# The sign of a weight word from ScalarE instead of VectorE, for 20 of 32 pieces

## The chip, the cores and the metric

The kernel runs on one core of a Trainium2 chip. The metric is the device time of one execution in microseconds, the median of several. The engines are TensorE (PE, matrix products), VectorE (DVE), ScalarE (ACT), GpSimd (POOL) and SyncE (SP, which here issues DMAs).

## What is computed

The reference is attention with a local window and a few global keys, then a two-layer network with a gelu:

```python
batch, n_heads, seq, head_dim = (4, 8, 768, 64)
n_tokens, d_model, d_ff = (3072, 512, 2048)
...
scores = scale * q @ k.T + bias        # bias: minus slope times distance
scores = where(is_global | is_local, scores, -1e9)
a = softmax(scores)
x = (a @ v)  as (3072, 512)
h = x @ w_in                            # (3072, 2048)
g = 0.5 * h * (1.0 + erf(h / sqrt(2)))
return (g @ w_out).astype(float32)
```

The weights w_in and w_out are 64-bit floats. The chip has none, so each weight arrives as two 32-bit words and has to be decoded into a 32-bit float, and then into two 16-bit floats (a high and a low part) for TensorE.

## The kernel before

The tokens go in 12 chunks of 256 (`NCH`), the 2048 columns of the hidden layer in 8 slices of 256 (`NST`). A step is one chunk with one slice: products with w_in, gelu, products with w_out. The method `run` walks over the steps and emits for each the products of the next step, the gelu, the attention of later chunks and the loads. The first two chunks are interleaved slice by slice, and while they run the weights are decoded; from the third chunk on all weights lie decoded in SBUF. The table `DECODE` says at which step each piece is decoded. The attention of a chunk consists of scores (`scores_pair`, reduced on VectorE in line 511), exponentials (`exps`, line 545, ScalarE), the reciprocal and the normalising (`norm`, lines 554 to 563; VectorE for the first two chunks, POOL for later ones), transposes (`flip`, line 584, TensorE, copied by ScalarE in line 589) and the products with v (`av_pair`, line 658), of which ScalarE makes the high half of x and VectorE the low half (line 212). Counted products of zeros (`FILL`, `warm`) keep TensorE busy between the products of the first attention.

A piece of weights is 128 x 512 words of 64 bits; there are 4 in a slice and 32 in all. `load_words` fetches it by SP (line 223) into one of 4 buffers of the pool `ws` or 3 of the pool `stg`. `split_weights` decodes it: the low word is scaled to a small integer in place (line 250 on POOL for slices 0 and 1, `s < POOLED`; line 252 on ScalarE for slices 2 to 7); VectorE shifts the high word's lower bits up (line 258), puts its two top bits in front (line 261) and adds the low word (line 263). A step later `part_weights` lets ScalarE make the high 16-bit part (line 273) and VectorE the low one (line 213).

The order on each engine is not the order of the text: a planner simulates the engines as it goes and places every instruction by that. The method `after` ties an instruction behind another without a wait; `behind` ties a VectorE instruction behind the last reduction of earlier steps, and `last_table` ties a ScalarE instruction behind the last exponential or gelu of earlier steps, because ScalarE loads another table (1.28 us in the trace) at each change between these two. Between engines, a reader of a tile waits by a semaphore for its writer.

Of the kernel before, what the change touches and what calls it, by code (L numbers as in the profile page):

```python
# [10 lines left out]
F16 = mybir.dt.float16  # L11
I32 = mybir.dt.int32
U32 = mybir.dt.uint32
AF = mybir.ActivationFunctionType
ALU = mybir.AluOpType
# [42 lines left out]
POOLED = 2  # L58
# [60 lines left out]
class Fast:  # L119
# [115 lines left out]
    def split_weights(self, s, i):  # L235
        nc = self.nc
        if i == 0:
            if s == LATE:
                self.early.close()
                self.wts = self.ctx.enter_context(self.tc.tile_pool(name="wlate", bufs=1, side="right"))  # L240
            if s == NST - 1:
                self.words.close()
                self.wts = self.ctx.enter_context(self.tc.tile_pool(name="wlast", bufs=1))
            for nm, dst, shape in (("win", self.win, [P, 4, 256]), ("wout", self.wout, [P, 2, 512])):
                dst[s] = tuple(self.wts.tile(shape, F16, name=f"{nm}{k}{s}") for k in "hl")
            self.sw[s] = self.wts.tile([P, 2, 4, 256], F16, name=f"sw{s}")
        w = self.raw.pop((s, i, "w"))
        lw, hw = w[:, :, 0], w[:, :, 1]
        if s < POOLED:
            nc.gpsimd.tensor_scalar(out=lw, in0=lw.bitcast(U32), scalar1=2.0 ** -29, scalar2=None, op0=ALU.mult)  # L250
        else:
            ins = nc.scalar.activation(out=lw, in_=lw.bitcast(U32), func=AF.Copy, scale=2.0 ** -29).ins
            if len(self.his) > 1:
                self.after(ins, self.his[-2], "a piece begins when ScalarE is through with the last but one")
            if self.last_table is not None:
                self.after(ins, self.last_table, "a piece comes behind the exponentials of earlier steps")
        a = self.sm.tile([P, 512], I32, name=f"wb{s}_{i}", tag="o", bufs=3)
        ins = nc.vector.tensor_scalar(out=a, in0=hw, scalar1=0x07FFFFFF, scalar2=3,
                                      op0=ALU.bitwise_and, op1=ALU.logical_shift_left)
        self.behind(ins)  # L260
        nc.vector.scalar_tensor_tensor(out=a, in0=hw, scalar=-0x40000000, in1=a,
                                       op0=ALU.bitwise_and, op1=ALU.bitwise_or)
        nc.vector.tensor_tensor(out=a, in0=a, in1=lw, op=ALU.add)  # L263
        self.words_of[s, i] = a

# [977 lines left out]
```

## Time and profile before

| | us |
|---|---|
| median of 3 runs | 616.1 (615.17, 616.1, 620.82) |
| profiled execution | 614.87 |
| its span, first to last instruction | 613.1 |
| PE busy | 594.8 (97%) |
| DVE busy | 478.6 (78%) |
| ACT busy | 351.2 (57%) |
| POOL busy | 94.3 (15%) |

The busy time is the share of the span in which an engine worked. TensorE's products are pipelined and their ends are modelled, so its busy time is no measure of how well it is used, but its idle time and what ended it can be read. The weights are decoded between 12 and 125 us of the span.

### The profile page before, as it was taken

To read this page: it belongs to the slowest core of one execution; us is meant where nothing else is said; L and a number is where in the kernel's file an instruction comes from. 1 tells how busy PE (TensorE), PEld (TensorE's weight loads), DVE (VectorE), ACT (ScalarE), POOL (GpSimd) and SP (SyncE) were. 2 spreads that over 40 slices of the span, in tenths; PEclk is the share of its full clock that TensorE was granted. 3 is DMA by queue.
4 is the path that set the end of the run, shared out by engine and by line. 5 is a ranking of instruction groups with operands and counts; after the bars stand their busy time and mean duration, and the time that the engine had idled before them with its cause. 6 is when DMAs were issued, how large, how long until landed. Compare 5 with 4: busy or idle time off the path is not lost.

```text
span 613.1 us, 18033 instructions
## 1 busy us (share of the span) xinstructions
PE 594.8 (97%) x7320; PEld 451.6 (74%) x7320; DVE 478.6 (78%) x1490; ACT 351.2 (57%) x817; POOL 94.3 (15%) x196
## 2 busy tenths in 40 slices
PE   8988999999999999999999999999999999999995
PEld 5655544445666666888888888888888888888884
DVE  7999999977658865767966966976976976975885
ACT  3686577685636736547557556556566466463331
POOL 2240006311303111022022022022022022020000
PEclk9999999999999999999999999999999999999999
DMA  8969826443531364183184184194294194100001
GB/s 260 236 235 257 274 96 207 113 78 104 127 79 52 77 154 120 44 217 122 41 220 124 37 223 122 70 220 127 72 218 129 69 212 136 69 3 2 35 1 40
DMA packets 106618, 77.00 MB, mean 126 GB/s; under 512 B 54176, under 2 KB 94112, under 8 KB 106528
## 3 DMA queue, kind: packets, MB, share of 16 engines
q1 hardware_dynamic: 103952, 72.11, 42.4%
q10 hardware_dynamic: 2576, 3.67, 1.8%
q8 instruction: 59, 0.97, 0.7%
q14 instruction: 31, 0.25, 0.1%
HBM read 69.47 MB, written 6.29 MB: 124 GB/s over the span
## 4 chain that ended last, share of the span: by engine, by line
PE 60%; DVE 21%; ACT 10%; DMA 4%; issue 2%; SPq 1%; POOL 1%; ACTq 0%; DVEq 0%; POOLq 0%
PE h L717 23%; PE seven L793 16%; PE acc L883 7%; ACT n L545 4%; PE av L615 4%; DVE ss L757 3%; PE s L449 3%; PE h L711 3%; PE acc L868 2%; DMA w<-w 2%; DMA kr<-kT 2%; ACT L545 2%; DVE x L212 2%; DVE gl L213 2%; DVE wb L263 1%
## 5 line engine op out<-in xcount | busy, mean ns | idle before, releaser
L717 PE MATMUL h<-x,winh 128*128 128x256 f16 x1344 | 225.7, 273 | 1.7 <-DVE x L212 1.7
L717 PE MATMUL h<-x,winl 128*128 128x256 f16 x672 | 183.1, 273 | 0.0
L717 PEld LDWEIGHTS <-winh 128*128 128x128 f16 x1344 | 129.2, 98 | 24.2 <-issue 4.0
L563 POOL TENSOR_SCALAR n<-n,su 128x160 f32<-128x160 f32 (+1 forms) x160 | 77.4, 504 | 411.3 <-DVE su L557 270.0
L759 ACT ACTIVATE sh<-ss 128x512 f16<-128x512 f32 x64 | 40.3, 630 | 70.5 <-DVE ss L757 70.5
L752 ACT ACTIVATE gr<-h 128x512 f32<-128x512 f32 x64 | 38.2, 597 | 65.8 <-PE h L717 63.1
L717 PEld LDWEIGHTS <-winl 128*128 128x128 f16 x672 | 65.8, 98 | 8.9 <-issue 1.3
L213 DVE SCALAR_TENSOR_TENSOR gl<-gr,gh 128x384 f16<-128x384 f32 (+1 forms) x96 | 57.4, 598 | 12.4 <-ACT gh L854 12.0
L793 PE MATMUL seven<-sw,sh 128*128 128x256 f16 x384 | 66.9, 273 | 0.0
L545 ACT ACTIVATE n<-n,mn 128x160 f32<-128x160 f32 x144 | 59.6, 415 | 1.8 <-DVE mn L460 1.6
L757 DVE TENSOR_TENSOR ss<-gr 128x128 f32<-128x128 f32 x128 | 31.1, 284 | 32.3 <-ACT gr L752 32.3
L793 PEld LDWEIGHTS <-sh 128*128 128x128 f16 x512 | 50.1, 98 | 5.8
L793 PE MATMUL seven<-sw,sl 128*128 128x256 f16 x192 | 52.3, 273 | 0.1
L213 DVE SCALAR_TENSOR_TENSOR sl<-ss,sh 128x512 f16<-128x512 f32 x64 | 44.1, 690 | 9.4 <-ACT sh L759 9.4
L460 DVE CUSTOM_DVE_ANT_0 n<-s,pens 128x160 f32<-128x160 f32 x144 | 37.9, 320 | 7.0 <-PE s L449 6.7
L793 PEld LDWEIGHTS <-gh 128*128 128x128 f16 x384 | 35.9, 98 | 9.4 <-ACT gr L752 3.3
L212 DVE TENSOR_TENSOR x<-av,x 128x256 f16<-128x256 f32 x41 | 15.3, 417 | 28.9 <-ACT x L628 28.7
L545 ACT ACT_TABLE_LOAD x22 | 28.2, 1283 | 12.6 <-DMA qr<-qT 6.7
L793 PE MATMUL seven<-wouth,gh 128*128 128x256 f16 x128 | 35.1, 274 | 0.0
L793 PE MATMUL seven<-wouth,gl 128*128 128x256 f16 x128 | 34.9, 273 | 0.0
L793 PE MATMUL seven<-woutl,gh 128*128 128x256 f16 x128 | 34.9, 273 | 0.0
L758 ACT ACTIVATE gh<-gr 128x384 f16<-128x384 f32 x64 | 33.5, 523 | 2.0
(168 smaller groups left out, 1185.1 us busy)
## 6 DMA issues: line engine op xcount, KB each, us to landing
w<-w SPq DMA_DIRECT2D x32, 512.0 KB, 5.8
c<-w SPq DMA_DIRECT2D x32, 512.0 KB, 4.3
kr<-kT SPq DMA_DIRECT2D x34, 320.0 KB, 4.9
qr<-qT SPq DMA_DIRECT2D x11, 512.0 KB, 4.2
kr<-kT SPq DMA_DIRECT2D x84, 64.0 KB, 4.3
vr<-v SPq DMA_DIRECT2D x24, 176.0 KB, 2.9
out<-o SPq DMA_DIRECT2D x14, 256.0 KB, 2.0
out<-o ACTq DMA_DIRECT2D x8, 256.0 KB, 2.0
```

Of the source, the lines that this page charges most:

```text
L212: return self.nc.vector.tensor_tensor(out=out, in0=in_, in1=hi, op=ALU.subtract)
L213: return self.nc.vector.scalar_tensor_tensor(out=out, in0=in_, scalar=scale, in1=hi, op0=ALU.mult, op1=ALU.subtract)
L460: ins = nc.vector.tensor_tensor_reduce(out=nn[:, 2 * hh + u], in0=sp[hh][:, u, :], in1=pens, scale=-0.125, scalar=3e38, op0=ALU.add, op1=A ...
L545: self.table(nc.scalar.activation(out=nn, in_=nn, func=AF.Exp, bias=mn[:, i:i + 1], scale=-1.0, accum_out=su[:, i:i + 1]))
L563: ins = eng.tensor_scalar(out=nn, in0=nn, scalar1=su[:, i:i + 1], scalar2=0.0, op0=ALU.mult, op1=ALU.add)
L717: ins = nc.tensor.matmul(hp[:, f, :], lhsT=w[:, d, fs], rhs=x[:, d, e, :], start=n == 0, stop=n == 3 * NP - 1).ins
L752: self.table(nc.scalar.activation(out=gr.rearrange("p i q -> p (i q)"), in_=hp.rearrange("p f q -> p (f q)"), func=AF.Gelu, scale=1.0 / (W ...
L757: self.last_sum = nc.vector.tensor_tensor(out=ss[:, o], in0=x, in1=y, op=op).ins
L758: nc.scalar.activation(out=gh, in_=gr[:, 1:], func=AF.Copy, scale=GS)
L759: self.last_table = nc.scalar.activation(out=sh, in_=ss, func=AF.Copy, scale=GS).ins
L793: ins = nc.tensor.matmul(out, lhsT=g, rhs=w, start=s == 0 and name in ("P1", "P4", "P6", "P3") and i == 0, stop=s >= NST - 4 and i == 2, s ...
L883: ins = nc.tensor.matmul(acc, lhsT=g[:, f, ks], rhs=w[:, f, :], start=s == 0 and n == 0, stop=s == NST - 1 and n == 5).ins
```

## The change

In `split_weights` the operation that puts the two top bits of the high word in front is kept for 12 pieces only: the even ones of slices 2 to 7. For the other 20 (all eight of slices 0 and 1, the odd ones of slices 2 to 7) ScalarE reads the high word as an integer, scales it by 2 to the minus 60 and writes the result as a 16-bit float. The result is too small for that format and becomes a zero with the sign of the word. It goes into the upper half of the low word, behind line 250 or 252, which has left zeros there. The addition of line 263 then brings in the sign together with the low word. The second-highest bit is left out; for these weights it is zero.

```diff
         ins = nc.vector.tensor_scalar(out=a, in0=hw, scalar1=0x07FFFFFF, scalar2=3,
                                       op0=ALU.bitwise_and, op1=ALU.logical_shift_left)
         self.behind(ins)
-        nc.vector.scalar_tensor_tensor(out=a, in0=hw, scalar=-0x40000000, in1=a,
-                                       op0=ALU.bitwise_and, op1=ALU.bitwise_or)
+        if s < POOLED or i % 2:
+            sign = w.rearrange("p f t -> p (f t)").bitcast(F16).rearrange("p (f t) -> p f t", t=4)[:, :, 1]
+            ins = nc.scalar.activation(out=sign, in_=hw, func=AF.Copy, scale=2.0 ** -60).ins
+            if self.last_table is not None:
+                self.after(ins, self.last_table, "a piece comes behind the exponentials of earlier steps")
+        else:
+            nc.vector.scalar_tensor_tensor(out=a, in0=hw, scalar=-0x40000000, in1=a,
+                                           op0=ALU.bitwise_and, op1=ALU.bitwise_or)
         nc.vector.tensor_tensor(out=a, in0=a, in1=lw, op=ALU.add)
```

## Rows read from the trace of the kernel before

**Rows 1.** Busy time by stretch: busy us (x instructions) by engine, TensorE clock, DMA.

```profile
9.40:19.70 10.30, 9.08 (x70) 5.92 (x68) 8.72 (x39) 6.66 (x28) 6.59 (x4) 1.00 1.08 332
19.70:28.40 8.70, 8.39 (x81) 5.59 (x82) 8.01 (x35) 6.91 (x26) 0.00 (x0) 1.00 0.83 178
28.40:37.30 8.90, 7.01 (x79) 5.01 (x79) 8.78 (x36) 6.11 (x16) 4.93 (x4) 1.00 1.00 363
37.30:48.20 10.90, 8.85 (x95) 5.36 (x95) 9.54 (x33) 8.92 (x27) 1.46 (x1) 1.00 0.30 95
48.20:60.00 11.80, 10.52 (x110) 7.54 (x111) 11.80 (x27) 7.70 (x15) 0.00 (x0) 1.00 1.04 289
60.00:98.10 38.10, 37.32 (x211) 18.16 (x208) 37.80 (x87) 25.01 (x52) 5.20 (x5) 1.00 0.56 178
98.10:150.00 51.90, 51.44 (x420) 26.89 (x421) 44.58 (x131) 35.28 (x80) 14.56 (x37) 1.00 0.48 132
150.00:560.00 410.00, 408.16 (x5815) 330.94 (x5814) 305.36 (x971) 237.62 (x551) 59.98 (x136) 1.00 0.43 116
```

**Rows 2.** TensorE's waits, 9.4 to 62 us: total us, times, longest us.

```profile
PE t L584 <- DVE n L563: 2.6, 3, 1.2
PE acc L883 <- DVE gl L213: 1.6, 2, 1.0
PE av L658 <- DVE su L557: 1.2, 1, 1.2
PE h L717 <- DVE x L212: 1.0, 2, 0.6
PE av L658 <- ACT pt L589: 0.3, 1, 0.3
```

**Rows 3.** Decoding instructions by line: ns shortest/median/longest, first and last start, form.

```profile
L261 DVE SCALAR_TENSOR_TENSOR wb<-w,wb x32: 671/684/1010, 16.3 to 120.8; 128x512 int32<-128x512 int32 x32
...
L252 ACT ACTIVATE w<-w x24: 657/675/715, 47.7 to 118.0; 128x512 int32<-128x512 uint32 x24
L250 POOL TENSOR_SCALAR w<-w x8: 1552/1576/1782, 12.0 to 37.1; 128x512 int32<-128x512 uint32 x8
```

**Rows 4.** The chain of waits, 9 to 62 us: start us, us, what.

```profile
16.27 1.01 DVE wb L261
...
28.86 0.60 DVE wb L261
...
33.32 0.60 DVE wb L261
...
40.92 0.59 DVE wb L261
```

**Rows 5.** ScalarE's timeline: start us, us, operation, idle time before it and its end.

```profile
17.52 0.40 ACT L545 ACTIVATE n<-n,nmax 128x128 f32<-128x128 f32 x1 [2.76 <-DVE nmax L511]
...
30.32 0.63 ACT L273 ACTIVATE wouth<-wb 128x512 f16<-128x512 f32 x1 [1.68 <-DVE wb L263]
...
35.66 1.28 ACT L850 ACT_TABLE_LOAD   x1
...
47.75 1.23 ACT L252 ACTIVATE w<-w 128x512 int32<-128x512 uint32 x2
...
118.01 0.69 ACT L252 ACTIVATE w<-w 128x512 int32<-128x512 uint32 x1 [1.50 <-DMA w<-w]
```

**Rows 6.** POOL's timeline, 9 to 48 us.

```profile
14.21 5.08 POOL L250 TENSOR_SCALAR w<-w 128x512 int32<-128x512 uint32 x3 [0.57 <-DMA w<-w]
32.13 6.62 POOL L250 TENSOR_SCALAR w<-w 128x512 int32<-128x512 uint32 x4 [12.84 <-DMA w<-w]
```

**Rows 7.** TensorE's waits, 62 to 130 us.

```profile
PE t L584 <- POOL n L563: 0.8, 1, 0.8
PE h L711 <- DVE x L212: 0.5, 1, 0.5
```

**Rows 8.** SP's queue, its waits, 0 to 130 us.

```profile
SPq L223 <- DVE wb L263: 46.0, 11, 14.8
```

## The prediction

> **What bounds the kernel now.** I read the busy time by stretch first, then TensorE's waits, then the chain of waits, then the timelines of ScalarE and POOL. From 150 us on TensorE is busy 408.16 of 410 us and no weight is decoded any more, and from 60 to 150 us it is busy all but 1.24 us [rows 1]. Nothing that VectorE or ScalarE is spared there can come back as time. What is open lies between 9.4 and 60 us: TensorE misses 1.22, 0.31, 1.89, 2.05 and 1.28 us in the five stretches, 6.75 in all, while VectorE is nearly full (11.80 of 11.80 in the last one) and ScalarE has 2 to 4 us to spare in each but the second, where 1.8 are left [rows 1]. The granted clock is 1.00, that is 2.4 GHz, in all of these stretches, so none of the missing time is a slow clock. Nearly every wait of TensorE there ends with a VectorE operation: reciprocal, normalised probabilities, the low halves of x and g; only 0.3 us end with a ScalarE copy [rows 2]. The chain that ended last runs through the operation that is taken out (line 261) again and again; four of its pieces before 48 us stand in [rows 4]. So before 60 us VectorE is what the start waits for, and the removed operation stands in its queue.
>
> **The change part by part.** Removed are 20 of the 32 operations of line 261, 0.684 us each at the median [rows 3] and 0.60 of the chain when they run back to back [rows 4]: all eight pieces of the first two slices, decoded before about 52 us, and the twelve odd pieces of the other six, decoded behind them. Added are 20 copies on ScalarE. No row shows one that reads 32-bit words at a stride of 8 bytes and writes 16-bit ones at that stride. The nearest is the copy of line 252, same words and same stride, 0.675 us [rows 3]; two of them in a row take 1.23 us, so one occupies the engine for 0.55 [rows 5]. The upper bound is the strided operation of POOL, 1.58 us [rows 3]. I take 0.55, as the same engine on the same tile. No DMA is moved. SP's weight loads wait 46.0 us in total for line 263, which frees the buffers [rows 8]; line 263 now waits for ScalarE's copy instead of line 261, and what is queued behind it on VectorE waits with it.
>
> First stretch, to 19.7 us: line 261 took 1.01 us there, directly ahead of the score reductions whose exponentials ScalarE stood idle 2.76 us for [rows 4, 5], and TensorE waits 1.2 us for the reciprocal behind them [rows 2]. The new copy needs POOL's first piece, done at 13.64 us (14.21 less 0.57 of idle time) [rows 6], and falls into those 2.76 us: cost nothing. If that cover were gone it would cost 0.55. Gain **1.0**. The operation is 0.33 longer here than its median, while POOL works without a break from 14.21 on [rows 3, 6]; I count the whole 1.01, an assumption: what moves into its place are score reductions with one operand in PSUM, and they may or may not be held up like it. The Trainium skill, page "SBUF — State Buffer" (its part on the two sides of the memory) speaks against that: VectorE and GpSimd lock a shared pair of ports, and an operation with two SBUF inputs or in a two-port mode blocks fully behind a GpSimd operation that reads SBUF, so the 0.33 would pass to the next such operation; the first term would then be 0.67 and the sum 0.3 smaller. The row at 1.01 fits a short wait and no row shows the full one.
>
> Second stretch, to 28.4 us: TensorE has only 0.31 to give back, and that wait is for a ScalarE copy of probabilities [rows 1, 2]. ScalarE is busy 6.91 of 8.7 us. Two or three of the new copies come up here; one may slip into the 1.68 us that stand idle after it [rows 5], one I put on the path. Loss **0.55** (bounds 0 and 1.1).
>
> Third stretch, to 37.3 us: VectorE is busy 8.78 of 8.90 and TensorE misses 1.89 us, behind the low half of x and the normalised probabilities [rows 1, 2]. Two operations of line 261 at 0.60 precede both [rows 4]. Gain **1.2** (bounds 0 and 1.89).
>
> Fourth stretch, to 48.2 us: two more, that at 40.92 and one like it, 1.2 us of VectorE [rows 4]; ScalarE is busy 8.92 of 10.90 and has the second group's signs, of which I put one on the path at 0.55. Gain **0.6** (bounds a loss of 0.5 and a gain of 2.05).
>
> Fifth stretch, to 60 us: VectorE is full, loses at least three of the operations (1.8 us), and TensorE misses only 1.28. Its larger wait is for the low half of g, which needs the gelu on ScalarE too, so I take two thirds. Gain **0.9** (bounds 0 and 1.28).
>
> Behind 60 us the twelve other operations lie beside a full TensorE. Its two waits are 0.8 us for POOL's probabilities and 0.5 us for x [rows 7]. An emptier VectorE can close the first; the copy for the last odd piece comes right behind line 252 at 118.01 [rows 5], in front of the x that the second wait is for, and can add 0.55. I count **0** (bounds a loss of 0.6 and a gain of 1.24).
>
> Sum: 1.0 - 0.55 + 1.2 + 0.6 + 0.9 = 3.2 us (3.15) less. The profiled execution took 614.87 us (span 613.1), which gives 611.7; the median of the runs, 616.1, gives 612.9. I say **612.3**, between them.
>
> **The rivals.** *Nothing moves.* The operations leave VectorE, but TensorE's waits are taken over by exponentials and copies on ScalarE, whose queue grows by about 0.55 for every 0.60 that VectorE loses, and the warm-up products that are counted out by hand stay. For it: the wait in the second stretch is ScalarE's already [rows 2]. Against it: ScalarE has 2 to 4 us free in four stretches. Time 614.9 to 616.1, say 615.5.
>
> *All of it comes back.* The planner sets the order anew, every copy falls into idle time, and TensorE's 6.75 us and the 1.24 behind them close: 614.87 - 8.0 = 606.9, with a little left over 608. For it: VectorE's relief before 60 us is about 10 x 0.6 = 6 us, near what is missing. Against it: the waits are in series with exponentials and DMA landings that do not get shorter.
>
> *Slower: ScalarE's queue stops behind POOL.* For the first two slices the new copy writes into the word that POOL has just written, so it must wait for POOL. The second group of four POOL operations runs from 32.13 to 38.75 us [rows 6], and ScalarE's chain of table loads, gelu and exponentials starts at 35.66 [rows 5]. If the planner's order puts the group's last copy ahead of that chain, the chain starts at about 38.75 + 0.68 = 39.4, 3.8 us late, and VectorE stands behind line 263 too. From 615.5 that is 619.3. It decides as soon as one copy of the group is queued ahead of the table load while its POOL operation is unfinished. If the first group (POOL until 19.29, exponentials at 17.52) does the same, 2.5 us more: 621.8. For it: an engine keeps its order, and POOL's 1.6 us a piece are long. Against it: each copy is tied behind the exponentials of an earlier step, and those of 17.52 us start well after POOL's first piece is done.
>
> **How the numbers follow.** Forecast 0.50, nothing moves 0.25, all of it 0.13, slower 0.12. The range 608 to 618.5 reaches from the full gain to a small stall; it leaves out the lowest tip (down to 606.9) and the larger stalls. A measurement tells about 1% from no change, here 6.2 us: faster than 609.9 are most of the full gain and a tip of the forecast, 0.13; slower than 622.3 takes both groups of the stall and more, 0.06; within, 0.81.
>
> **What would show it.** In the changed kernel: 12 operations of line 261 instead of 32; copies of 0.6 to 0.7 us on ScalarE; the exponentials of 17.52 us about 1 us earlier; TensorE's waits for VectorE between 9.4 and 60 us at some 3 us in place of 6.4; the stretch behind 150 us of the same length, moved. Wrong if ScalarE's waits name line 250, if line 263 waits for ScalarE, if TensorE's waits before 60 us add up to 6 us or more, or if TensorE's waits behind 60 us change by over 1 us.

## The result and the profile after

The changed kernel is slower. The median of its runs is 625.43 us (624.87 to 628.42, 4 runs) against 617.55 us (615.17 to 620.82, 4 runs) of the kernel before, taken beside it; the ratio is 1.0146, 95% interval [1.0111, 1.0181]. The profiled execution took 625.88 us, its span is 624.0 us, 10.9 more than before. VectorE is busy 469.2 us in place of 478.6 and ScalarE 373.3 in place of 351.2. From line 263 of the kernel before on, lines are numbered 6 higher here (line 589 is 595, line 717 is 723); line 263 is now the sign copy and line 269 the addition.

The operation that was added, by its line (ns shortest/median/longest, first and last start, form), stands against the row of line 252 in [rows 3], which was taken for its price:

```profile
L263 ACT ACTIVATE w<-w x20: 1322/1346/1407, 14.3 to 119.5; 128x512 f16<-128x512 int32 x20
```

It is twice as long as that copy: 1.35 us. The busy time by stretch, in the columns of [rows 1] (us; PE, PEld, DVE, ACT and POOL busy with counts; TensorE's clock; DMA):

```profile
9.40:19.70 10.30, 8.89 (x67) 5.81 (x67) 8.17 (x38) 7.16 (x27) 6.48 (x4) 1.00 1.08 329
19.70:28.40 8.70, 6.94 (x56) 4.40 (x55) 6.92 (x28) 7.35 (x20) 0.18 (x1) 0.80 0.90 188
28.40:37.30 8.90, 7.40 (x87) 5.28 (x81) 7.46 (x28) 5.56 (x18) 5.23 (x3) 1.00 0.96 353
37.30:48.20 10.90, 8.99 (x114) 5.78 (x113) 6.67 (x25) 10.52 (x24) 1.71 (x2) 1.00 0.29 97
48.20:60.00 11.80, 8.67 (x42) 5.28 (x41) 9.19 (x29) 10.98 (x25) 0.00 (x0) 0.73 0.66 182
```

VectorE is no longer full in any of these stretches. ScalarE is nearly full in the last two rows, 10.52 of 10.90 and 10.98 of 11.80. TensorE's idle time in these five stretches is 9.71 us, up from 6.75, and two rows have a granted clock below 1.00, which none in [rows 1] had. TensorE's waits from 9.4 to 62 us, in the columns of [rows 2]:

```profile
PE av L664 <- ACT pt L595: 5.4, 4, 1.7
PE t L590 <- DVE n L569: 1.9, 2, 1.6
PE h L723 <- ACT x L689: 1.8, 1, 1.8
PE t L528 <- DVE x L212: 0.4, 1, 0.4
```

In [rows 2] ScalarE ended 0.3 us of 6.7; here it ends 7.2 of 9.5. Its timeline (start us, us, operation, idle time before it) shows what stands ahead of the first of them:

```profile
14.32 1.35 ACT L263 ACTIVATE w<-w 128x512 f16<-128x512 int32 x1 [0.67 <-POOL w L250]
15.42 0.95 ACT L595 COPY pt<-t 128x384 f32<-128x384 f32 x2
18.10 0.41 ACT L551 ACTIVATE n<-n,nmax 128x128 f32<-128x128 f32 x1 [1.74 <-DVE nmax L517]
...
19.77 0.61 ACT L279 ACTIVATE winh<-wb 128x512 f16<-128x512 f32 x1
20.29 1.33 ACT L263 ACTIVATE w<-w 128x512 f16<-128x512 int32 x1
21.37 0.57 ACT L595 COPY pt<-t 128x384 f32<-128x384 f32 x1
```

A sign copy stands right in front of the copies of transposed probabilities (line 595). Before, no such copy stood there, and the exponentials that started at 17.52 us [rows 5] start at 18.10. TensorE in the same place:

```profile
21.99 0.43 PE L664 MATMUL av<-pt,vr 128*64 128x128 f32 x2 [1.72 <-ACT pt L595]
22.35 1.17 PE L504 MATMUL s<-kr,qr 64*128 64x128 f32 x12
23.45 2.07 PE L535 MATMUL warm_ps<-wz 128*128 128x512 f32 x4
```

The wait of 1.72 us ends at 21.99; the four products of zeros behind it take 2.07 us, where four elsewhere in this trace, at 17.32, take 1.19. The granted clock, in windows of 2 us, is 0.75, 0.50 and 0.89 from 22 to 28 us and 0.93, 0.50, 0.50, 0.50 and 0.86 from 52 to 62: TensorE's lower level, 1.2 GHz. It fell after stretches in which TensorE stood for much of the time (0.28 us busy of 2 from 20 to 22 us; 1.24 and 0.85 of 2 each from 50 to 54), and it rose again while TensorE worked. Other stretches as idle were followed by no fall (0.64 us busy of 2 from 14 to 16, 0.50 from 32 to 34, 0.36 from 38 to 40). One minus the clock, times the 2 us of each of these windows, adds up to 5.1 us: TensorE ran at half rate for some 10.3 us and got 5.1 us less work done in them.

Most of the loss arises at the start. Of the 10.9 us, 8.9 are there at the last product of the two interleaved chunks with w_out (line 868; the times before the semicolon are the first and the last start). Before:

```profile
L868 PE MATMUL acc<-wouth,gh x48: 379/379/390, 75.7 to 145.7; 128*128 128x512 f16 x48
```

After:

```profile
L874 PE MATMUL acc<-wouth,gh x48: 379/379/390, 83.4 to 154.6; 128*128 128x512 f16 x48
```

### The profile page after: what moved, and what is told of

It is laid out like the page before. It is cut to its first block, busy times and chain, and to the rows that moved or that the text cites. A ratio compares the mean times of both kernels' runs of the same rounds, so it can differ in the third digit from the quotient of the medians.

```text
span 624.0 us, 18031 instructions
## 1 busy us (share of the span) xinstructions
PE 599.2 (96%) x7320; PEld 454.2 (73%) x7320; DVE 469.2 (75%) x1470; ACT 373.3 (60%) x837; POOL 90.3 (14%) x196
## 4 chain that ended last, share of the span: by engine, by line
PE 54%; DVE 21%; ACT 16%; DMA 3%; issue 3%; SPq 2%; DVEq 0%; ACTq 0%
PE h L723 22%; PE seven L799 15%; PE acc L889 6%; ACT n L551 5%; PE av L621 4%; DVE ss L763 3%; PE s L455 3%; SPq L333 2%; DVE gl L213 2%; DVE ptb L581 2%; DVE x L212 2%; ACT L551 2%; ACT w L263 1%; DMA w<-w 1%; DVE o L812 1%
## 5 line engine op out<-in xcount | busy, mean ns | idle before, releaser
L569 POOL TENSOR_SCALAR n<-n,su 128x160 f32<-128x160 f32 (+1 forms) x160 | 72.5, 474 | 429.2 <-DVE su L563 282.9
L213 DVE SCALAR_TENSOR_TENSOR gl<-gr,gh 128x384 f16<-128x384 f32 (+1 forms) x96 | 57.3, 597 | 11.8 <-ACT gh L860 11.1
```

What stands on the lines that cost most here:

```text
L213: return self.nc.vector.scalar_tensor_tensor(out=out, in0=in_, scalar=scale, in1=hi, op0=ALU.mult, op1=ALU.subtract)
L569: ins = eng.tensor_scalar(out=nn, in0=nn, scalar1=su[:, i:i + 1], scalar2=0.0, op0=ALU.mult, op1=ALU.add)
```

## The experiments

The first theory: the copy costs more than twice what was assumed and stands in front of copies that TensorE waits for. Its rivals: the planner, which orders every engine anew, has made a worse order whatever the copy costs; or TensorE's clock falls, and that is what costs.

**forms.** A small kernel of its own times the copy in nine shapes, four of each, most of them taking turns with another shape. Of 512 elements, 16-bit results are written 8 bytes apart (tb, te, tf, th), 4 bytes apart (td) or close together (hc), and 32-bit ones 8 bytes apart (ta, tg).

```diff
+    act = lambda o, x, s: nc.scalar.activation(out=o, in_=x, func=AF.Copy, scale=s)
...
+            act(half(t["b"], 1, 4), hi, 2.0 ** -60)
```

> Not the computation: a small program that runs ScalarE's copy of 128 x 512 elements in nine forms, four times each, and adds the results into the output so that nothing is left out. Theory A (the new copy is dear because it writes 16-bit words at a stride): every form with a strided 16-bit output takes about 1.33 us, with any input; a contiguous 16-bit output from the same strided integers takes 0.61 to 0.68, and strided 32-bit output 0.66 to 0.68. Rival B (it is dear because of the integer input, or because the result underflows): a contiguous output from the same integers with the same scale also takes about 1.3, and the strided output whose scale gives ordinary numbers is cheap. Rival C (it is dear only beside the other engines' work): all forms take 0.6 to 0.7 here.

The groups by line (x count | busy us, mean ns | idle us):

```profile
L123 ACT ACTIVATE tf<-flat 128x512 f16<-128x512 int32 x4 | 5.6, 1391 | 0.0
...
L123 ACT ACTIVATE tb<-src 128x512 f16<-128x512 int32 x4 | 5.3, 1320 | 0.0
L123 ACT ACTIVATE th<-src 128x512 f16<-128x512 f32 x4 | 5.3, 1318 | 0.0
L123 ACT ACTIVATE td<-src 128x512 f16<-128x512 int32 x4 | 3.1, 766 | 0.0
L123 ACT ACTIVATE tg<-src 128x512 int32<-128x512 int32 x4 | 2.8, 705 | 0.0
...
L123 ACT ACTIVATE hc<-src 128x512 f16<-128x512 int32 x4 | 2.6, 648 | 0.0
```

The read does not matter (tf reads close together and is no shorter), nor the conversion (hc converts as well, in 0.65 us), nor the stride alone (tg writes 32 bits at the same stride in 0.70 us). What costs is 16-bit results written 8 bytes apart. Ordinary numbers in place of signed zeros (te) took 1.37 us. The Trainium skill, page "ScalarE: Activation LUTs", section "What ACT_TABLE_LOAD costs", gives an ACTIVATE with immediate scale and bias 186 ns and 0.833 ns for each element, fp32 and bf16 alike; an estimate by it for 512 elements is 613 ns. The measurement is near it, at 642 to 705 ns, for four of the shapes, and is twice as long for this one; the measurement decides.

**early** and **late.** One part of the change alone: the first eight pieces, or the twelve later ones.

```diff
-        if s < POOLED or i % 2:
+        if s < POOLED:                 # early
+        if s >= POOLED and i % 2:      # late
```

> ScalarE's sign for the eight pieces of slices 0 and 1 alone; the other 24 stay with VectorE. Theory A (the loss arises before about 62 us, where the copies stand in front of the copies of probabilities that TensorE waits for): most of the loss is here, ratio to the kernel before 1.010 to 1.016, TensorE's clock falls once or twice before 62 us. Rival D (ScalarE's load in all of the decoding is the loss, in proportion): 8 of 20, ratio 1.005 to 1.007.

> ScalarE's sign for the twelve odd pieces of slices 2 to 7 alone; the first eight stay with VectorE. Theory A: TensorE is full from 60 us on, so ratio 0.997 to 1.003. Rival D (load in proportion): 12 of 20, ratio 1.007 to 1.010.

early is 1.0142 [1.0115, 1.0170], the whole loss, with 5.5 us of waits for the copies of probabilities. late is 1.0050 [1.0025, 1.0074], above what the first theory gave it: its clock stays at 1.00, but TensorE waits 2.4 us for a gelu behind 98 us. A loss in proportion to the number of copies fits neither.

**cheap.** The sign copy becomes one that costs as much as line 252, in the same place on every engine. This kernel leaves the sign out, as do drop below and all that are built on it, and it never takes the second path that a flag at the end can start.

```diff
-            ins = nc.scalar.activation(out=sign, in_=hw, func=AF.Copy, scale=2.0 ** -60).ins
+            ins = nc.scalar.activation(out=lw, in_=lw.bitcast(U32), func=AF.Copy, scale=1.0).ins
```

> The changed kernel with the sign copy replaced by a copy of the low word onto itself, 32-bit, the form of line 252 (0.67 us in place of 1.35), at the same places: the sign of the weights is left out, and the flag that would start the second path is multiplied by zero. Every engine's order is the same as in the changed kernel. Theory A1 (the price of the copy makes the loss): 20 x 0.67 us of ScalarE's queue go, the four waits for probabilities shrink by 0.5 to 0.7 each and the clock stays up; ratio to before 1.000 to 1.005. Rival E (the new order makes it, whatever the copy costs): ratio 1.011 to 1.016.

The copies took 0.67 us (638/669/702 ns), and the ratio is 1.0075 [1.0043, 1.0107], between the two expectations. At about the price that the prediction assumed the change is still a loss, half as large.

**tied.** The sign copies, and with them the two top bits of the other pieces and all additions, are emitted at the end of the step; the copies are tied behind those of the step.

```diff
+            if self.last_copy is not None:
+                self.after(ins, self.last_copy, "behind the copies of the step")
...
+            for args in self.signs:
+                self.sign_weights(*args)
```

> The changed kernel, all 20 copies at their full price of 1.35 us, but each is given out after the step's copies of probabilities and x and tied behind the last of them; line 263's addition follows it. Theory A (the loss is the copies' place in front of what TensorE waits for, and the price sets how much): TensorE's waits for ScalarE's copies before 62 us fall from 7.2 to under 4 us, the clock does not fall there, ratio 1.000 to 1.007. Rival D (ScalarE is simply overloaded): ratio 1.010 to 1.016, as in the changed kernel.

It is 1.0162 [1.0117, 1.0206]. TensorE's waits for the copies of probabilities fall to 2.6 us, as meant, but waits for gelu halves and normalised probabilities take their place, and the granted clock falls three times. So taking the sign copies out of the way of those copies is not enough; the order changed with it once more.

**load.** VectorE keeps all of its 32 operations and the copies come on top, writing plain zeros (the edit is against the changed kernel).

```diff
-            ins = nc.scalar.activation(out=sign, in_=hw, func=AF.Copy, scale=2.0 ** -60).ins
+            ins = nc.scalar.activation(out=sign, in_=hw.bitcast(U32), func=AF.Copy, scale=2.0 ** -60).ins
...
-        else:
-            nc.vector.scalar_tensor_tensor(out=a, in0=hw, scalar=-0x40000000, in1=a,
...
+        nc.vector.scalar_tensor_tensor(out=a, in0=hw, scalar=-0x40000000, in1=a,
...
```

> VectorE keeps its operation in all 32 pieces and ScalarE has the 20 copies on top, of the high word read as unsigned, so that they write plain zeros. Theory A (what VectorE is spared gives nothing back while ScalarE holds the start up): ratio 1.013 to 1.019, as in the changed kernel or a little over. Rival G (VectorE's relief did give 3 to 4 us back and the copies cost 12 to 13): ratio 1.019 to 1.024.

It is 1.0123 [1.0072, 1.0174], not to be told from the change itself: VectorE's relief has shown nowhere so far.

**drop.** The 20 operations go and nothing comes in their place.

```diff
         if s < POOLED or i % 2:
-            sign = ...
-            ins = nc.scalar.activation(out=sign, in_=hw, func=AF.Copy, scale=2.0 ** -60).ins
+            pass
```

> VectorE's operation is taken out of the 20 pieces and nothing put in its place: the sign of these weights is left out, and the flag that would start the second path is multiplied by zero. The forecast's gain without any cost: 4.3 us less by its first, third, fourth and fifth stretch, ratio 0.991 to 0.995. Rival F (TensorE's start waits for a chain of exponentials, copies and products that VectorE's relief does not shorten): ratio 0.997 to 1.003.

It is 1.0031 [1.0007, 1.0055]. A kernel with 20 instructions less and nothing added is not faster. The clock falls twice, at 20 to 26 and 62 to 68 us, and 3.1 us of TensorE's waits are for copies of probabilities, though ScalarE has nothing new to do. That points to the order.

**fill.** More products of zeros, with the planner free to order.

```diff
-FILL_T = {(1, 6): 6}
+FILL_T = {(1, 6): 14}
+MORE = {(0, 3): 6, (1, 4): 0}
```

> The changed kernel with more products of zeros where TensorE waits for the copies of probabilities: six more in the first attention and eight more in the second. Theory H (a good part of the loss, 3 to 4 us, is TensorE at 1.2 GHz behind waits of 1.7 and 2.7 us): the granted clock stays at 1.00 before 62 us and the ratio falls from 1.0146 to 1.007 to 1.011. Rival: the waits cost what they cost and the slow products are hidden by the next wait; ratio 1.013 to 1.017 with the clock at 1.00.

It is 1.0157 [1.0124, 1.0190]. The clock holds to 66 us and falls from there to 74. No gain; but the order changed again.

**zero** and **pin_drop.** The same work in two orders. All that is emitted is recorded; then every instruction of an engine is tied behind the one that a given order puts before it, so that the planner has no choice left. The code is that of zero, cut.

```diff
             fast.run(flag_i)
+            pin(fast)
...
+        for x, y in zip(seq, seq[1:]):
+            fast.after(y, x, "the order of the changed kernel")
```

zero has the order of the changed kernel, with the 20 copies left out. pin_drop has that of the kernel before, with the 20 operations of VectorE left out. Both run the same instructions, those of drop. In the traces VectorE, ScalarE and POOL have exactly the orders that were given, less what is left out; TensorE's differs from them in a few records behind 270 us.

> The changed kernel in exactly its own order on every engine, held by ties, with the 20 copies left out: their price is 0 where the run with the cheap copy had 0.67 us and the changed kernel 1.35 us. The sign of these weights is left out and the flag that would start the second path is multiplied by zero. Theory A1 (at one order the loss is the price, about linear): ratio 0.999 to 1.002. Theory E1 (the order alone costs some us, whatever the copies cost): ratio 1.004 to 1.008, with TensorE's clock at 1.2 GHz at least once before 70 us.

> VectorE's operation taken out of the 20 pieces and nothing put in its place, as in an earlier run, but every engine held in the order of the kernel before by ties. The sign of these weights is left out and the flag is multiplied by zero. Theory J (the forecast's gain was there and the new order ate it): ratio 0.991 to 0.996, the clock at 1.00 throughout. Rival F (VectorE's relief shortens nothing that TensorE waits for in any order): ratio 0.998 to 1.002.

zero is 1.0084 [1.0068, 1.0100] (621.57 us), pin_drop 0.9904 [0.9890, 0.9918] (610.99 us). One set of instructions, two orders, 1.8% between them: some 11 us. This is the answer to where the gain went. Most of it shows in TensorE's products of the interleaved chunks with w_out, first in pin_drop, then in zero:

```profile
L872 PE MATMUL acc<-wouth,gh x48: 379/379/390, 72.5 to 140.5; 128*128 128x512 f16 x48
...
L871 PE MATMUL acc<-wouth,gh x48: 379/379/390, 80.1 to 149.9; 128*128 128x512 f16 x48
```

The last of them starts 9.4 us later in zero. From 9.4 us to there TensorE is idle for 8.1 us in zero and 3.5 in pin_drop, and busy for 132.3 and 127.6 us with the same products, which zero runs in part at the lower clock: half of the difference is waiting, half is the clock.

In the order of before the relief of VectorE is worth 0.96%, some 5.9 us, more than forecast. The busy rows of pin_drop:

```profile
9.40:19.70 10.30, 10.07 (x76) 6.70 (x77) 8.81 (x44) 7.63 (x30) 6.28 (x4) 1.00 1.07 329
...
48.20:60.00 11.80, 11.13 (x113) 8.03 (x113) 10.81 (x22) 8.96 (x17) 0.00 (x0) 1.00 1.16 299
60.00:98.10 38.10, 38.10 (x207) 17.89 (x205) 34.40 (x81) 25.70 (x54) 5.96 (x8) 1.00 0.56 180
```

and those of zero:

```profile
9.40:19.70 10.30, 9.34 (x69) 6.08 (x69) 7.91 (x40) 6.62 (x28) 6.55 (x4) 1.00 1.09 334
19.70:28.40 8.70, 8.21 (x63) 5.50 (x63) 7.57 (x31) 4.88 (x17) 0.00 (x0) 0.80 0.83 190
28.40:37.30 8.90, 6.74 (x83) 4.47 (x81) 6.57 (x26) 6.46 (x24) 5.08 (x4) 1.00 0.99 371
37.30:48.20 10.90, 10.01 (x99) 6.36 (x100) 7.04 (x25) 7.03 (x16) 1.55 (x1) 0.84 0.23 74
48.20:60.00 11.80, 10.07 (x93) 6.96 (x92) 10.40 (x31) 9.16 (x23) 0.00 (x0) 0.86 0.74 206
```

The clock reads 1.00 in every row of pin_drop and is below it in three of zero. cheap has the order of zero, by the planner itself and not by ties; at 1.0075 its copies cost nothing that can be measured, and neither do the ties: its loss was the order. (The kernel before, tied to its own order, was not run.)

**pin_sign** and **pin_free.** The whole change, its 20 copies at 1.35 us, in the order of before, each copy put by hand into ScalarE's order where that engine stood idle, as far as it did (for two pieces of slice 1 it did not); pin_free leaves the four pieces of slice 1 to VectorE.

```diff
+PLACE = {(0, 0): 15, (0, 1): 23, (0, 2): 38, ...}   # piece: position in ScalarE's order
...
-        if s < POOLED or i % 2:
+        if s == 0 or s >= POOLED and i % 2:     # pin_free
```

> The change complete (20 copies at 1.35 us on ScalarE, 20 operations off VectorE), every engine held in the order of the kernel before, and each copy put by hand where ScalarE stood idle in the trace of before, as far as there is such a place; for slice 1 there is none for two of the four. Theory J with the price of slice 1 (about 2 us): ratio 0.995 to 1.002 and no fall of the clock. Rival D (ScalarE is overloaded in any order): ratio 1.008 to 1.016.

> As the run before, but the four pieces of slice 1, for which ScalarE has no free place, stay with VectorE: 16 copies. Theory J: ratio 0.993 to 0.998, faster than the kernel before by 1 to 4 us. Rival D: ratio 1.004 to 1.012; rival F: 0.999 to 1.003.

pin_sign is 0.9969 [0.9950, 0.9988] (615.43 us) and pin_free 0.9976 [0.9961, 0.9992]. Both beat the kernel before, by 1.9 and 1.5 us, and the kernel after by some 10; the intervals come close to 1. pin_sign's copies, and its products of the interleaved chunks with w_out, of which the last starts 1.1 us earlier than before:

```profile
L265 ACT ACTIVATE w<-w x20: 1328/1355/1430, 14.8 to 118.1; 128x512 f16<-128x512 int32 x20
...
L874 PE MATMUL acc<-wouth,gh x48: 379/379/390, 75.2 to 144.6; 128*128 128x512 f16 x48
```

**zero_warm** and **after_warm.** Is it the clock that the order costs, or the waits? Both keep the order of the changed kernel and put more products of zeros into TensorE's idle stretches.

```diff
+MORE_T = {(1, 2): 4, (1, 3): 2, (1, 6): 7}              # zero_warm, before the transposes of a head
+MORE_W = {(0, 3): 4}                                    # behind them
+MORE_T = {(1, 2): 7, (1, 6): 7}                         # after_warm
+MORE_W = {(0, 1): 4, (0, 3): 6, (0, 7): 5}
```

> As zero (the changed kernel's order on every engine, no sign copies; the low words lack their sign and the flag at the end is zeroed), with 17 more zero products on TensorE, put into the three idle stretches that stood ahead of the falls of the granted clock: four products behind the transposes before the wait of 1.30 us at 18.9 to 20.2, six in the waits at 36 to 38, seven more in the wait of 1.61 us at 50.2 to 51.8. The engine's order is else the same. Theory K (the order costs mostly through the clock: about 5.1 us of TensorE's time was granted at half rate between 20 and 56): the granted clock stays at 1.00 up to 80 us, and the ratio to the kernel before falls from 1.0084 to 1.000 to 1.004. Theory W (the order costs by its waits, and the clock only fills time in which TensorE would wait anyway): the clock stays up or nearly, and the ratio stays at 1.006 to 1.010.

> The changed kernel in its own order on every engine, the 20 copies with it, and 29 more zero products in the idle stretches of TensorE: 4, 6 and 5 behind the transposes ahead of the waits of 1.15, 1.72 and 1.50 us at 16, 22 and 33 us, 7 in the wait of 1.81 us at 40, 7 in that of 1.62 us at 53. Theory K: the clock stays at 1.00 up to 80 us and the ratio falls from 1.0146 to 1.006 to 1.010, by most of the 5.1 us that were granted at half rate. Theory W: the ratio stays at 1.012 to 1.017, clock or not.

zero_warm is 1.0054 [1.0028, 1.0079], between the two expectations, and its clock is 1.00 in every stretch up to 150 us:

```profile
19.70:28.40 8.70, 7.24 (x68) 4.97 (x69) 7.58 (x31) 4.67 (x18) 0.00 (x0) 1.00 0.86 181
...
48.20:60.00 11.80, 11.41 (x114) 8.96 (x115) 11.40 (x33) 10.85 (x26) 0.00 (x0) 1.00 0.79 230
```

Against zero that is 0.3%, some 2 us, with intervals that overlap; against pin_drop 1.5% are left. But this does not tell what the clock costs. In the profiled execution (622.71 us) TensorE is busy for 131.9 us up to the last product with w_out and idle for 8.2, nearly the 132.3 and 8.1 of zero: the 17 added products took about the time that the higher clock saved. after_warm is 1.0130 [1.0088, 1.0172], not to be told from the change, and says less: its clock still falls from 56 to 60 us, and its added products wait 2.3 us for a copy of probabilities.

**only_act, only_pe, only_dve.** Which engine's order holds the gain? The work of drop, with one engine tied to the order of before.

```diff
     for e, text in ORDER.items():
+        if e != "Activation":      # "PE", "DVE"
+            continue
```

> As pin_drop (the 20 VectorE operations left out, nothing put in for them, so that the low words lack their sign and the flag is zeroed), but only ScalarE's instructions are tied to the order of the kernel before; the planner orders the other engines anew. With every engine tied it was 0.9904, with none 1.0031. Theory A (the new order costs because exponentials and window copies stand ahead of the copies of probabilities on ScalarE): the ratio is 0.988 to 0.995. Theory P (it is TensorE's order, where the products of the first pieces are placed between the heads) and theory V (VectorE's order): 0.999 to 1.006.

> As only_act, with only TensorE's instructions tied to the order of the kernel before. Theory P: 0.988 to 0.995. Theories A and V: 0.999 to 1.006.

> As only_act, with only VectorE's instructions tied to the order of the kernel before (without the 20 removed). Theory V: 0.988 to 0.995. Theories A and P: 0.999 to 1.006. If none of the three alone comes below 0.995, the gain needs the orders of several engines together.

They are 0.9990 [0.9966, 1.0014], 1.0012 [0.9988, 1.0036] and 0.9998 [0.9978, 1.0018]; drop, with none tied, is 1.0031 and pin_drop, with all, 0.9904. None of the three theories is borne out. Tied ScalarE or VectorE bring the waits for copies of probabilities from 3.1 down to 0.3 us and hold the clock at 1.00 up to 150 us, tied TensorE does neither; but no one of them brings the gain, so it needs the orders of several engines together. Which of them was not tried.

## Why the prediction was wrong

**The loss in three parts.** By the ratios to the kernel before: the relief of VectorE in its order is -0.96% (pin_drop); the new order, with the same work, +1.80% (zero against pin_drop); the copies in that order +0.62% (the change against zero). They add up to the +1.46% measured by the way they are taken; each is uncertain by 0.2 to 0.4%. In microseconds at 617: -5.9, +11.1 and +3.8. In the order of before the copies cost much the same, +0.65% (pin_sign against pin_drop), so they cost some 4 us of the 27 that they occupy in either. In the change they cost TensorE waits alone: up to its last product with w_out it is idle for 12.8 us, after 8.1 in zero, and busy for 132.4, after 132.3.

**The step that failed first** is one that the sum never wrote down: it priced each edit against the timeline of before, as if every other instruction stayed in its place. The text that describes the kernel says that a planner places each instruction anew, and the prediction used that in two rivals only: in its favour, where all comes back, and for the place of one copy behind POOL. No rival had the new order of everything else as a loss. It was the largest term, some 11 us. Why the planner's new order came out worse was not examined.

**The price of the copy** was taken at 0.55 us from line 252 [rows 3, 5]; it is 1.35 alone, and two in a row take 2.48 us, so by the same reckoning one occupies the engine for 1.13. The bound from POOL, 1.58, held. Two terms of 0.55 were put on the path, 1.1 us in all; pin_sign against pin_drop is 2.6 us behind at the first product of slice 2 with w_in (line 711 of before; 63.9 against 61.3 us) and 4.1 at the last product with w_out (144.6 against 140.5).

**The first stretch** was right for the order of before. In both pinned kernels the exponentials of 17.52 us [rows 5] start 0.97 and 1.00 us earlier. ScalarE's timeline in pin_drop:

```profile
16.55 0.40 ACT L549 ACTIVATE n<-n,nmax 128x128 f32<-128x128 f32 x1 [1.22 <-DVE nmax L515]
```

and in pin_sign, where the sign copy lies in the idle time, as said:

```profile
14.76 1.38 ACT L265 ACTIVATE w<-w 128x512 f16<-128x512 int32 x1
...
16.52 0.40 ACT L551 ACTIVATE n<-n,nmax 128x128 f32<-128x128 f32 x1 [0.38 <-DVE nmax L517]
```

The smaller term that the Trainium skill's page "SBUF — State Buffer", section "🔬 SBUF: two separate sides", would have given did not come. VectorE's timeline in pin_drop shows the shift, right behind it the score reductions that moved up, and then the addition, while POOL works:

```profile
15.89 0.41 DVE L259 TENSOR_SCALAR wb<-w 128x512 int32<-128x512 int32 x1
16.23 0.28 DVE L515 CUSTOM_DVE_ANT_0 n<-s,pens 128x128 f32<-128x128 f32 x1
...
16.44 0.35 DVE L515 CUSTOM_DVE_ANT_0 n<-s,pens 128x192 f32<-128x192 f32 x1
...
17.21 0.88 DVE L267 CUSTOM_DVE_ANT_0 wb<-w,wb 128x1024 uint16<-128x1024 uint16 x1
```

The reductions are not held up. The addition, with two inputs in SBUF, is: 0.88 us, where it takes 0.68 while POOL rests (22.49 us). So a delay passed to the next operation of that kind, as the prediction had it from the page, but behind the reductions, and the exponentials start about as early as forecast. It was short: the addition ends at 18.09 us, inside an operation of POOL (16.89 to 18.45 us), so the full block of which the page speaks does not show here, and the measurement decides. In pin_sign another operation is hit:

```profile
15.43 0.86 DVE L259 TENSOR_SCALAR wb<-w 128x512 int32<-128x512 int32 x1
```

The same shift takes twice as long, but the reductions still start in time.

**Stretches one to five in sum** came out with the right sign and three quarters of the size, in the order of before. The first product of slice 2 with w_in (line 711, 64.4 us before) starts at 61.3 us in pin_drop: 3.1 us earlier, where the prediction's terms without its two for the copies give 4.25.

**Behind 60 us** the prediction was wrong. By the last product with w_out pin_drop is 5.2 us ahead (140.5 for 145.7), so 2.1 us came back where it counted 0 and had a bound of 1.24. By the starts of the same products in the two traces they came back at just the two waits of [rows 7]: 1.2 us at the wait for POOL's probabilities and 0.8 at that for x, each 0.3 to 0.4 us more than the wait that the profile shows. The prediction named both and counted neither, and its bound, TensorE's idle time, was too low: a busy TensorE was no proof that nothing is to be had.

**The slower rival** had the right sign and the wrong place: ScalarE waited for POOL's word once, 0.7 us. The table load of 35.66 us [rows 5] came at 42.06 all the same, behind exponentials that the new order put ahead of it, a sign copy and copies of probabilities.

All four signs that were to show the prediction wrong came: ScalarE's waits name line 250 (0.7 us), the addition waits for ScalarE's copy (0.7 us), TensorE's waits up to 62 us are 9.5 us, and those from there to 150 us 3.1, after 1.3 in the kernel before. With the order kept, the change takes 615.43 us: 3.1 more than forecast, and inside the range, but in part by luck, as the relief was worth 5.9 us instead of 4.25 and the copies cost 4.0 instead of 1.1.

## What to carry to other kernels

Where a planner orders the instructions, an edit is two changes, and the second can be the larger: pin the old order and measure the edit in it before you judge it, and then search the order. The price of a copy is that of its exact output form: time the one that you mean to add, above all where narrow results are written apart. Taking instructions out can cost time (drop, 1.0031) when the order changes with it. And a run that fills idle time to hold the clock up also pays for what it fills in.

## What the runs showed of the hardware

ScalarE writes 512 16-bit results per partition in 0.65 us close together, 0.77 at 4 bytes apart and 1.32 at 8 bytes apart, and 32-bit ones at 8 bytes apart in 0.70.

TensorE's granted clock went from 1.00 to 0.50 after stretches in which TensorE mostly waited, though not after every such stretch, and at different places in the new orders (from 22 us in the change, 40 in cheap, 30 in tied, 16 in load); zero products that ran at half rate took 2.07 us instead of 1.19. In zero TensorE idles 4.7 us more than in pin_drop and works 4.7 us longer on the same products. Holding the clock up with added products, in zero_warm, gave back only about 2 of some 11 us, as they took about as long as the clock had cost. What a clock held without them would give back, and which waits of the new order cost the rest, is not settled.
